# An up product in two slices at a time: four full passes and four 32-row tiles in place of eight full passes

## The chip, the cores and the metric

The kernel runs on one core of a Trainium2 chip. The metric is the device time of one execution in microseconds (us), as the median of several runs. A smaller number is better.

## What is computed

Agent attention over 4 batches of 12,480 tokens with 128 channels and 49 agents, followed by a feed-forward layer of 2,048 hidden units over all 49,920 tokens. All data are float32 (q, k and the agents are drawn eight times larger than v). Cut to what matters:

```python
a2k = softmax(scale * agents @ k.T)      # 49 x 12480 per batch
agent_v = a2k @ v                        # 49 x 128
q2a = softmax(scale * q @ agents.T)      # 12480 x 49
x = q2a @ agent_v                        # tokens x 128
h = x @ w_in                             # 128 -> 2048
g = h * sigmoid(1.702 * h)
out = g @ w_out                          # 2048 -> 128
```

## The kernel before

**What is multiplied.** The 128 channels between the attention and the feed-forward layer are never formed. For each batch the kernel computes `agent_v @ w_in` once, a 49 x 2048 matrix, and uses it as the weights of the up product; the moving operand of that product is the softmax of a token over the 49 agents. The output is computed transposed, channels on partitions.

**Two parts for each operand.** The matmuls run on the reduced type float32r. To keep float32 accuracy, each operand is split into an upper part (the value rounded to float32r) and a lower part (what is left), and a product is the sum of up to three products of parts. In the up product the split of the softmax costs no extra pass: rows 0 to 48 of the 128 contraction rows hold the upper part of 49 agents, rows 64 to 112 the lower part, and the weights `wh` are repeated in both places. Rows 49 to 63 and 113 to 127 are zero and do nothing. The lower part of the weights, `wl`, is a second pass over the same moving operand.

**Tiles.** Tokens go in groups of 960 (`GT`), two chunks of 480 (`CH`): 13 groups in each of 4 batches, 52 in all. The 2,048 hidden units go in 16 slices of 128 (`NF`). A step is one slice of one group, so there are 832 steps. In each step, on TensorE:

- `up` (L391): two accumulators `ph` of 128x480 in PSUM (of four), and four matmuls of 480 columns: `wh` with each chunk (`sa`, `sb`; L396), `wl` with each chunk (L398). ScalarE then applies GELU from each `ph` into `g` (L401).
- `high` (L404): the upper part `gh` of `g`, by a casting DMA from GpSimd's queue in 6 slices of 16 (L407), by ScalarE in 8 (L409), by VectorE in 2 (L411). `low` (L414): `gl = g - gh` on VectorE (L416).
- `down` (L419), five steps later (`LAG`): six matmuls of 480 columns into the two `po` accumulators (L427): `wo_h` with `gh`, `wo_h` with `gl`, `wo_l` with `gh`, for two chunks.

**What runs beside it.** Jobs are put at steps by hand (`put(step, job)`) and run between `up` and `down` of the step. For the next group: the query scores at steps 4 and 5 (`Q_AT`; `scores`, L181: 16 small bf16 matmuls for each half, then a VectorE reduction that adds the two halves of each score, L196), the shift by the maximum, the exponential on ScalarE at step 8 (`E_AT`, L358), the sums at 10, the softmax into `p_pad` at 11, and at step 13 (`P_AT`) `query_pairs` (L375): four transposes on TensorE (L379), then ScalarE copies the upper parts into `sa` and `sb` and VectorE writes the lower parts. For the next batch: key loads, splits and scores, the key maximum (two small transposes, L245 with 120 contraction rows and L255 with 49), then v (`value_hi`, L284, and `value_lo`, L288, on VectorE), the product with v (L292), and last `weights_part` (L329), which makes `wh` and `wl` (L335 to L337), 512 columns at a time.

**Order.** Each engine runs its instructions in program order. From step 16 on the order on TensorE, ScalarE, VectorE and GpSimd is exactly the written one. The SP queue issues all loads and stores, also in order; GpSimd's queue issues the casting DMAs.

Of the kernel before, what the change touches and what calls it, by code (L numbers as in the profile page):

```python
# [8 lines left out]
F32 = mybir.dt.float32  # L9
# [25 lines left out]
HI_ON_ACT = (0, 2, 4, 6, 7, 12, 13, 15)  # L35
# [4 lines left out]
def kernel(  # L40
# [51 lines left out]
    p_pad = []  # L92
    for i in range(2):
        t = const.tile([P, CH // TB, P], F32, name=f"p_pad{i}")
        nc.gpsimd.memset(t, 0.0)
        p_pad.append(t)


    e_sb = []
    for i in range(2):  # L100
        t = const.tile([P, KB, A + 1], F32, name=f"e_sb{i}")
        nc.gpsimd.memset(t[:, :, A:], EPS)
        e_sb.append(t)
# [77 lines left out]
    def scores(b, parts, out, c):  # L181
        x0, x1, x2 = parts
        a = ag_part[:, b].rearrange("p i a -> p (i a)")
        mm = nc.tensor.matmul
        ps = ps_m.tile([P, 512], F32, name="ps_m")
        for j in range(KB // 2):
            t0 = (c * KB // 2 + j) * TB
            t = slice(t0, t0 + P)
            o = ps[:, j * 2 * A : (j + 1) * 2 * A]
            mm(out=o, lhsT=x0[:, t], rhs=a[:, 0 : 2 * A], start=True, stop=False)  # L190
            mm(out=o[:, A:], lhsT=x0[:, t], rhs=a[:, 2 * A :], start=False, stop=False)  # L191
            mm(out=o, lhsT=x1[:, t], rhs=a[:, 0 : 2 * A], start=False, stop=False)  # L192
            mm(out=o[:, 0:A], lhsT=x2[:, t], rhs=a[:, 0:A], start=False, stop=True)  # L193
        s = ps[:TB, : KB * A].rearrange("p (j i a) -> p j a i", i=2, a=A)
        o = out[:, c * KB // 2 : (c + 1) * KB // 2, :]
        nc.vector.tensor_reduce(out=o, in_=s, axis=AX.X, op=ALU.add)  # L196
# [29 lines left out]
    def key_scores(b, g, parts, c):  # L226
        scores(b, parts, score[:TB, g * KB : (g + 1) * KB, :], c)
# [55 lines left out]
    def value_hi(g, vt):  # L283
        nc.vector.tensor_copy(out=v_pair[:TB, :, 0:C], in_=vt[:TB])  # L284
# [43 lines left out]

    def weights_part(b, w, c):  # L329
        if c == 0:  # L330
            wts[b] = wpool.tile([P, F], F32R, name="wh"), wpool.tile([P, F], F32R, name="wl")
        wh, wl = wts[b]
# [3 lines left out]
        nc.scalar.copy(out=wh[:, s], in_=pw)  # L336
        nc.vector.tensor_sub(out=wl[:, s], in0=pw, in1=wh[:, s].bitcast(F32))  # L337


    def query_load(b, g):  # L340
        t = loads.tile([P, GT + PAD], F32, name="qt", tag="qt", bufs=2)
        nc.sync.dma_start(out=t[:, 0:GT], in_=qT[b, :, g * GT : (g + 1) * GT])
        return t

    def query_scores(n, b, parts, c):
        sd = e_sb[n % 2][:TB, :, 0:A]
        scores(b, parts, sd, c)
        return sd
# [11 lines left out]
    def query_sums(n):  # L360
        z = work.tile([P, KB], F32, name="z")
        nc.vector.tensor_reduce(out=z[:TB], in_=e_sb[n % 2][:TB], axis=AX.X, op=ALU.add)
        nc.vector.reciprocal(out=z[:TB], in_=z[:TB])
        return z

    def query_softmax(n, e, z):
        pp = p_pad[n % 2]
        nc.vector.tensor_tensor(
            out=pp[:TB].rearrange("p i (c x) -> p c i x", c=2)[:, :, :, 0:A],
            in0=e.rearrange("p (c i) a -> p c i a", c=2),  # L370
            in1=z[:TB].rearrange("p (c i) -> p c i", c=2).unsqueeze(3).broadcast_to([TB, 2, KB // 2, A]),
            op=ALU.mult,
        )

    def query_pairs(g):  # L375
        pp = p_pad[g % 2]
# [7 lines left out]
        nc.scalar.copy(out=sa[0:H], in_=ps[0:H, :CH])  # L384
        nc.scalar.copy(out=sb[H:P], in_=ps[H:P, :CH])
        nc.vector.tensor_sub(out=sa[H:P], in0=ps[0:H, :CH], in1=sa[0:H].bitcast(F32))
        nc.vector.tensor_sub(out=sb[0:H], in0=ps[H:P, :CH], in1=sb[H:P].bitcast(F32))
        return sa, sb


    def up(f, wts, pairs):  # L391
        wh, wl = wts
        s = slice(f * P, (f + 1) * P)
        ph = [ps_h.tile([P, 512], F32, name="ph") for _ in range(2)]
        for c in range(2):
            nc.tensor.matmul(out=ph[c][:, :CH], lhsT=wh[:, s], rhs=pairs[c], start=True, stop=False)  # L396
        for c in range(2):
            nc.tensor.matmul(out=ph[c][:, :CH], lhsT=wl[:, s], rhs=pairs[c], start=False, stop=True)  # L398
        g = gpool.tile([P, 2, CH], F32, name="g", bufs=LAG)
        for c in range(2):  # L400
            nc.scalar.activation(out=g[:, c, :], in_=ph[c][:, :CH], func=AF.Gelu_apprx_sigmoid)  # L401
        return g

    def high(f, g):  # L404
        gh = gpool.tile([P, 2, CH], F32R, name="gh", bufs=LAG + 1)
        if f in HI_ON_DMA:
            nc.gpsimd.dma_start(out=gh, in_=g)  # L407
        elif f in HI_ON_ACT:
            nc.scalar.copy(out=gh, in_=g)  # L409
        else:  # L410
            nc.vector.tensor_copy(out=gh, in_=g)  # L411
        return gh

    def low(g, gh):  # L414
        gl = gpool.tile([P, 2, CH], F32R, name="gl", bufs=LAG - 1)
        nc.vector.tensor_sub(out=gl, in0=g, in1=gh.bitcast(F32))  # L416
        return gl

    def down(f, gp, po):  # L419
        gh, gl = gp  # L420
        for lhsT, rhs, first, last in (
# [4 lines left out]
            for c in range(2):  # L426
                nc.tensor.matmul(  # L427
                    out=po[c][:, :CH],
                    lhsT=lhsT[:, f, :],
                    rhs=rhs[:, c, :],  # L430
                    start=(f == 0 and first),
                    stop=(f == NF - 1 and last),
                )
# [15 lines left out]
    scored = {}  # L449
    sums = {}  # L450
# [27 lines left out]
    def do_key_scores(b, g, c):  # L478
        key_scores(b, g, k_parts[b, g], c)
# [9 lines left out]
    def do_query_scores(n, c):  # L489
        if n < B * NG:  # L490
            b, g = divmod(n, NG)
            scored[n] = query_scores(n, b, q_parts[n], c)
# [23 lines left out]
    def first_keys():  # L516
        tags = [("g", LAG), ("gh", LAG + 1), ("gl", LAG - 1)]
# [10 lines left out]
    for g in range(NKG):  # L528
        if g % 2 == 0:
            vt0 = wpool.tile([P, 2, KB, C + 1], F32, name="vt0", tag=("wh", "wl")[g // 2 % 2])  # L530
# [11 lines left out]
    do_query_scores(0, 0)  # L542
    do_query_scores(0, 1)
# [54 lines left out]
    for b in range(B - 1):  # L598
        s0 = b * per_batch
        for k in range(NKG):  # L600
            t = pe_step(s0 + (10 if b == 0 else K_AT) + 5 * k)
            t1 = pe_step(t + 1)
            put(t - 13 if b else max(t - 13, 0), lambda b=b, k=k: do_key_load(b + 1, k))
            for i in range(4):
                put(t - 5 + i, lambda b=b, k=k, i=i: do_key_split(b + 1, k, i))
            put(t, lambda b=b, k=k: do_key_scores(b + 1, k, 0))
            put(t1, lambda b=b, k=k: do_key_scores(b + 1, k, 1))
            put(t1 + 1, lambda k=k: key_part_max(k))
        mx = {}
        put(t1 + 2, lambda mx=mx: key_max_0(mx))  # L610
        t = pe_step(t1 + 4)
        put(t, lambda mx=mx: key_max_1(mx))
        t = pe_step(t + 3)
        put(t, lambda mx=mx: key_max_2(mx))
        shift = t + 2


        g0 = (shift + 3 - s0 - E_AT + NF - 1) // NF
        for k in range(NKG):
# [6 lines left out]
            put(t - 3, lambda b=b, k=k: value_hi(k, vts[b + 1, k]))  # L626
# [36 lines left out]
    def step(t):
        if t < steps:
            n, f = divmod(t, NF)
            g = up(f, wts[n // NG], pairs[n])
            if f == NF - 1:
                pairs.pop(n)
        for job in at.pop(t, ()):
            job()  # L670
        if t < steps:
            gh = high(f, g)

            if f in HI_ON_DMA:
                at.setdefault(t + 3, []).insert(0, lambda t=t: live.update({t: (gh, low(g, gh))}))
            else:
                live[t] = gh, low(g, gh)
        if t >= LAG:
            n, f = divmod(t - LAG, NF)
            if f == 0:  # L680
                po[n] = [ps_o.tile([P, 512], F32, name=f"po{c}") for c in range(2)]
            down(f, live.pop(t - LAG), po[n])
            if f == NF - 1:
                store(*divmod(n, NG), po.pop(n))

    for t in range(NF):
        step(t)
# [42 lines left out]
```

## Time and profile before

| | |
|---|---|
| median of 3 runs | 2118.99 us (2118.6 to 2119.08) |
| the profiled execution | 2118.66 us, of which the span of the profile is 2116.9 us |
| granted TensorE clock, mean | 0.994 |
| ScalarE busy | 1563.2 us, 74% |
| DMA issues of `gh` | 312 of 480 KB, median 2.8 us to landing |
| first matmul of the up product, last matmul | at 75.16 and 2112.0 us |

The profile is one execution on the core. A row of the timeline gives the start in us from the span's beginning, the duration, the engine (PE is TensorE's matmul, PEld its weight load, DVE is VectorE, ACT ScalarE, POOL GpSimd, SPq the SP queue), the line, the operation, output and inputs, and in brackets the idle time before and what ended it. Matmul durations overlap: the distance from start to start tells what one costs. A row of the groups gives the busy time of all instructions of a line and form, the mean of one in ns, and the idle time before them.

### The profile page before, as it was taken

To read this page: it belongs to the slowest core of one execution; us is meant where nothing else is said; L and a number is where in the kernel's file an instruction comes from. 1 tells how busy PE (TensorE), PEld (TensorE's weight loads), DVE (VectorE), ACT (ScalarE), POOL (GpSimd) and SP (SyncE) were. 2 spreads that over 40 slices of the span, in tenths; PEclk is the share of its full clock that TensorE was granted. 3 is DMA by queue.
4 is the path that set the end of the run, shared out by engine and by line. 5 is a ranking of instruction groups with operands and counts; after the bars stand their busy time and mean duration, and the time that the engine had idled before them with its cause. 6 is when DMAs were issued, how large, how long until landed. Compare 5 with 4: busy or idle time off the path is not lost.

```text
span 2116.9 us, 32655 instructions
## 1 busy us (share of the span) xinstructions
PE 2085.7 (99%) x12232; PEld 1769.1 (84%) x12232; DVE 1741.0 (82%) x2259; ACT 1563.2 (74%) x2524; POOL 195.9 (9%) x436
## 2 busy tenths in 40 slices
PE   7899999999999999999999999999999999999999
PEld 7678888888888888888888888888888888888887
DVE  6899989888789988888879998888787777777775
ACT  3566777777777777777777777777777877878786
POOL 3000000000010000000001000000000000000100
PEclk9999999999999999999999999999999999999999
DMA  9533433433333433433323443433423333232322
GB/s 266 163 125 126 154 108 122 131 122 131 112 113 131 150 122 112 131 122 126 127 103 126 146 132 111 131 122 122 131 94 103 106 109 113 103 122 94 112 94 84
DMA packets 94276, 262.01 MB, mean 124 GB/s; under 512 B 9245, under 2 KB 35165, under 8 KB 94117
## 3 DMA queue, kind: packets, MB, share of 16 engines
q0 software_dynamic: 44928, 153.37, 20.4%
q1 hardware_dynamic: 49188, 106.55, 17.7%
q8 instruction: 96, 1.57, 0.3%
q14 instruction: 64, 0.52, 0.1%
HBM read 80.97 MB, written 25.56 MB: 50 GB/s over the span
## 4 chain that ended last, share of the span: by engine, by line
PE 92%; DVE 6%; DMA 1%; issue 1%; ACT 0%; ACTq 0%; SPq 0%; DVEq 0%; POOLq 0%
PE po L427 50%; PE ph L396 16%; PE ph L398 16%; PE ps_m L292 2%; DVE gl L416 2%; PE ps_m L190 2%; PE ps_m L192 1%; PE ps_m L209 1%; PE ps_m L379 1%; PE ps_m L191 1%; PE ps_m L193 1%; PE ps_m L335 1%; DMA words<-w_out 0%; DVE rest L175 0%; DVE v_pair L288 0%
## 5 line engine op out<-in xcount | busy, mean ns | idle before, releaser
L401 ACT ACTIVATE g<-ph 128x480 f32<-128x480 f32 x1664 | 854.4, 573 | 467.6 <-PE ph L398 434.0
L416 DVE TENSOR_TENSOR gl<-g,gh 128x960 fp32r<-128x960 f32 x832 | 951.1, 1156 | 249.6 <-ACT gh L409 200.0
L427 PE MATMUL po<-gh,wo_h 128*128 128x480 f32 x1664 | 524.5, 396 | 0.2 <-ACT o L438 0.2
L427 PE MATMUL po<-gh,wo_l 128*128 128x480 f32 x1664 | 501.8, 383 | 0.0
L427 PE MATMUL po<-gl,wo_h 128*128 128x480 f32 x1664 | 498.1, 381 | 2.2 <-DVE gl L416 2.2
L409 ACT CAST gh<-g 128x960 fp32r<-128x960 f32 x416 | 415.3, 998 | 12.3
L427 PEld LDWEIGHTS po<-gl,wo_h 128*128 128x128 f32 x1664 | 313.3, 188 | 52.3 <-DVE gl L416 2.3
L427 PEld LDWEIGHTS po<-gh,wo_l 128*128 128x128 f32 x1664 | 313.7, 189 | 49.3
L407 POOL DMA_DIRECT2D gh<-g x312 | 167.8, 538 | 1836.7 <-ACT g L401 1163.5
L427 PEld LDWEIGHTS po<-gh,wo_h 128*128 128x128 f32 x1664 | 292.7, 189 | 39.9 <-issue 5.7
L396 PE MATMUL ph<-sb,wh 128*128 128x480 f32 x832 | 319.5, 384 | 0.0
L396 PE MATMUL ph<-sa,wh 128*128 128x480 f32 x832 | 318.7, 383 | 0.6 <-ACT g L401 0.4
L398 PE MATMUL ph<-sa,wl 128*128 128x480 f32 x832 | 317.5, 382 | 0.0
L398 PE MATMUL ph<-sb,wl 128*128 128x480 f32 x832 | 315.9, 380 | 0.0
L396 PEld LDWEIGHTS ph<-sb,wh 128*128 128x128 f32 x832 | 157.5, 189 | 31.7 <-ACT g L401 5.3
L396 PEld LDWEIGHTS ph<-sa,wh 128*128 128x128 f32 x832 | 157.6, 189 | 29.9 <-ACT g L401 1.0
L398 PEld LDWEIGHTS ph<-sb,wl 128*128 128x128 f32 x832 | 156.6, 188 | 25.2 <-issue 0.2
L398 PEld LDWEIGHTS ph<-sa,wl 128*128 128x128 f32 x832 | 156.5, 188 | 24.5 <-issue 0.2
L177 DVE TENSOR_TENSOR rest<-rest 128x488 bf16<-128x488 f32 (+1 forms) x182 | 130.2, 721 | 0.6
L192 PE MATMUL ps_m<-ag_part,rest 128*128 128x98 bf16 x728 | 114.9, 205 | 0.0
L193 PE MATMUL ps_m<-ag_part,rest 128*128 128x49 bf16 x728 | 111.4, 187 | 0.0
L196 DVE TENSOR_REDUCE e_sb<-ps_m 120x196 f32<-120x392 f32 x104 | 58.9, 566 | 37.0 <-PE ps_m L193 36.9
(103 smaller groups left out, 1830.9 us busy)
## 6 DMA issues: line engine op xcount, KB each, us to landing
gh<-g POOLq DMA_DIRECT2D x312, 480.0 KB, 2.8
kt<-kT SPq DMA_DIRECT2D x52, 480.0 KB, 3.7
qt<-qT SPq DMA_DIRECT2D x52, 480.0 KB, 4.4
vt<-v SPq DMA_DIRECT2D x52, 480.0 KB, 4.2
outT<-o SPq DMA_DIRECT2D x104, 240.0 KB, 2.2
words<-w_in SPq DMA_DIRECT2D x4, 512.0 KB, 11.0
words<-w_out SPq DMA_DIRECT2D x4, 512.0 KB, 8.4
ag_sb<-agT SPq DMA_DIRECT2D x1, 98.0 KB, 2.0
```

Source lines behind the costliest of these rows:

```text
L177: nc.vector.tensor_sub(out=halves(r)[1][:, s], in0=r[:, s], in1=halves(r)[0][:, s])
L190: mm(out=o, lhsT=x0[:, t], rhs=a[:, 0 : 2 * A], start=True, stop=False)
L192: mm(out=o, lhsT=x1[:, t], rhs=a[:, 0 : 2 * A], start=False, stop=False)
L193: mm(out=o[:, 0:A], lhsT=x2[:, t], rhs=a[:, 0:A], start=False, stop=True)
L196: nc.vector.tensor_reduce(out=o, in_=s, axis=AX.X, op=ALU.add)
L396: nc.tensor.matmul(out=ph[c][:, :CH], lhsT=wh[:, s], rhs=pairs[c], start=True, stop=False)
L398: nc.tensor.matmul(out=ph[c][:, :CH], lhsT=wl[:, s], rhs=pairs[c], start=False, stop=True)
L401: nc.scalar.activation(out=g[:, c, :], in_=ph[c][:, :CH], func=AF.Gelu_apprx_sigmoid)
L407: nc.gpsimd.dma_start(out=gh, in_=g)
L409: nc.scalar.copy(out=gh, in_=g)
L416: nc.vector.tensor_sub(out=gl, in0=g, in1=gh.bitcast(F32))
L427: nc.tensor.matmul(out=po[c][:, :CH], lhsT=lhsT[:, f, :], rhs=rhs[:, c, :], start=(f == 0 and first), stop=(f == NF - 1 and last),)
```

## The change

The up product is made for two slices at once, and most of the lower weights move into the rows that were zero.

- `R = 30` agents: the 15 zero rows 49 to 63 of `wh` now hold the lower weights of agents 0 to 14, the zero rows 113 to 127 those of agents 15 to 29; `sa` and `sb` hold the upper softmax of these agents there. So the pass with `wh` also makes 30 agents' products with the lower weights.
- The lower weights of the last 19 agents go into `wq`, four times over, at rows 0, 32, 64 and 96; `rq` holds the upper softmax of these agents in the same rows, chunk 0 in row groups 0 and 2, chunk 1 in 1 and 3. After the four full passes of two slices (two slices by two chunks), four matmuls with 19 rows each, at tile positions (0,0), (32,0), (64,0), (96,0), finish the four `ph`, one tile each. All four `ph` of PSUM are thus in use at once.
- The rows are filled by DMAs inside SBUF, issued by SP (`move`): eight for each group of tokens in `query_pairs`, six for each of the four `weights_part` of a batch. The product with the lower part of the softmax and the lower weights, which the old second pass made too, is left out.
- A step pair runs `up` of two slices, the jobs of the first, `high` of the first and `low` of the slice two before, `high` of the second, `down` of the odd and then the even slice four steps earlier, with the jobs of the second step and its `low` between them.
- Even slices get `gh` by DMA (8 of 16); ScalarE does 6 odd ones, VectorE slices 7 and 9.
- `scores`: ScalarE copies one half of the scores out of PSUM, and VectorE adds the other a step later (instead of one reduction by VectorE).
- `value_hi` becomes a casting DMA from DRAM on GpSimd's queue.
- Jobs are placed anew (`P_AT` 10, `E_AT` 6, `Q_AT` 2 and others), and single buffers replace pairs for `p_pad`, `e_sb` and the query loads.

```diff
-LAG = 5
+LAG = 4
+G_BUFS = 5
+GH_BUFS = 6
+GL_BUFS = 4
-Q_AT = 4
-E_AT = 8
-P_AT = 13
-S_AT = 15
-K_AT = 4
-V_AT = 1
-V2_AT = 11
+Q_AT = 2
+E_AT = 6
+P_AT = 10
+S_AT = 13
+K_AT = 3
+V_AT = 0
+V2_AT = 9
+R = 30
-HI_ON_DMA = (1, 3, 5, 10, 11, 14)
-HI_ON_ACT = (0, 2, 4, 6, 7, 12, 13, 15)
+HI_ON_ACT = (1, 3, 5, 11, 13, 15)
...
-        s = ps[:TB, : KB * A].rearrange("p (j i a) -> p j a i", i=2, a=A)
+        s = ps[:TB, : KB * A].rearrange("p (j i a) -> p j i a", i=2, a=A)
-        nc.vector.tensor_reduce(out=o, in_=s, axis=AX.X, op=ALU.add)
+        nc.scalar.copy(out=o, in_=s[:, :, 0, :])
+        return lambda: nc.vector.tensor_add(out=o, in0=s[:, :, 1, :], in1=o)
...
-    def value_hi(g, vt):
-        nc.vector.tensor_copy(out=v_pair[:TB, :, 0:C], in_=vt[:TB])
+    def value_hi(b, g):
+        nc.gpsimd.dma_start(out=v_pair[:TB, :, 0:C], in_=v[b, :, g * KB : (g + 1) * KB, :])
...
         nc.scalar.copy(out=wh[:, s], in_=pw)
-        nc.vector.tensor_sub(out=wl[:, s], in0=pw, in1=wh[:, s].bitcast(F32))
+        wl = work.tile([P, 512], F32R, name="wl")
+        nc.vector.tensor_sub(out=wl[:A], in0=pw[:A], in1=wh[:A, s].bitcast(F32))
+        move(wh[A:H, s], wl[0 : R // 2])
+        move(wh[H + A : P, s], wl[R // 2 : R])
+        for i in range(4):
+            move(wq[i * 32 : i * 32 + A - R, s], wl[R:A])
+
+    def move(out, in_):
+        nc.sync.dma_start(out=out.bitcast(F32), in_=in_.bitcast(F32))
...
+        rq = work.tile([P, CH], F32R, name="rq")
+        hi = sa[0:A], sb[H : H + A]
+        lo = sa[H : H + A], sb[0:A]
+        parts = ps[0:A, :CH], ps[H : H + A, :CH]
+        for c in range(2):
+            nc.scalar.copy(out=hi[c], in_=parts[c])
+        for c, t in enumerate((sa, sb)):
+            nc.vector.tensor_sub(out=lo[c], in0=parts[c], in1=hi[c].bitcast(F32))
+            move(t[A:H], hi[c][0 : R // 2])
+            move(t[H + A : P], hi[c][R // 2 : R])
+            for i in (c, c + 2):
+                move(rq[i * 32 : i * 32 + A - R], hi[c][R:A])
+        return sa, sb, rq
...
     def up(f, wts, pairs):
-        for c in range(2):
-            nc.tensor.matmul(out=ph[c][:, :CH], lhsT=wh[:, s], rhs=pairs[c], start=True, stop=False)
-        for c in range(2):
-            nc.tensor.matmul(out=ph[c][:, :CH], lhsT=wl[:, s], rhs=pairs[c], start=False, stop=True)
+        wh, wq = wts
+        rq = pairs[2]
+        tiles = [(i, c) for i in range(2) for c in range(2)]
+        cols = [slice((f + i) * P, (f + i + 1) * P) for i in range(2)]
+        ph = [ps_h.tile([P, 512], F32, name="ph") for _ in tiles]
+        for k, (i, c) in enumerate(tiles):
+            nc.tensor.matmul(out=ph[k][:, :CH], lhsT=wh[:, cols[i]], rhs=pairs[c], start=True, stop=False)
+        for k, (i, c) in enumerate(tiles):
+            r = slice(k * 32, k * 32 + A - R)
+            nc.tensor.matmul(
+                out=ph[k][:, :CH],
+                lhsT=wq[r, cols[i]],
+                rhs=rq[r],
+                start=False,
+                stop=True,
+                tile_position=(k * 32, 0),
+            )
...
+    def two_steps(t):
+        n, f = divmod(t, NF)
         if t < steps:
+            g[t], g[t + 1] = up(f, wts[n // NG], pairs[n])
+        jobs(t)
+        if t < steps:
+            gh[t] = high(f, g[t])
+        if 2 <= t < steps + 2:
+            gl[t - 2] = low(g.pop(t - 2), gh[t - 2])
+        if t < steps:
+            gh[t + 1] = high(f + 1, g[t + 1])
+        for i in (1, 0):
+            if t >= LAG:
+                m, f = divmod(t - LAG + i, NF)
...
+                down(f, gh.pop(t - LAG + i), gl.pop(t - LAG + i), po[m])
+            if i:
+                jobs(t + 1)
+                if t < steps:
+                    gl[t + 1] = low(g.pop(t + 1), gh[t + 1])
```

More of the change, by code (lines that the diff above doesn't have):

```diff
@@ L91 @@
     nc.gpsimd.memset(v_pair[:, :, 2 * C :].bitcast(F32), 1.0)
[L92 to L103, printed above, removed]
+    p_pad = const.tile([P, CH // TB, P], F32, name="p_pad")
+    nc.gpsimd.memset(p_pad, 0.0)
+    e_sb = const.tile([P, KB, A + 1], F32, name="e_sb")
+    nc.gpsimd.memset(e_sb[:, :, A:], EPS)
     w_in_sb = const.tile([P, F], F32, name="w_in_sb")
@@ L226, in key_scores @@
     def key_scores(b, g, parts, c):
-        scores(b, parts, score[:TB, g * KB : (g + 1) * KB, :], c)
+        return scores(b, parts, score[:TB, g * KB : (g + 1) * KB, :], c)
     def key_part_max(g):
@@ L330, in weights_part @@
         if c == 0:
-            wts[b] = wpool.tile([P, F], F32R, name="wh"), wpool.tile([P, F], F32R, name="wl")
-        wh, wl = wts[b]
+            wts[b] = wpool.tile([P, F], F32R, name="wh"), wpool.tile([P, F], F32R, name="wq")
+        wh, wq = wts[b]
         s = slice(c * 512, (c + 1) * 512)
@@ L336, in weights_part @@
         nc.scalar.copy(out=wh[:, s], in_=pw)
-        nc.vector.tensor_sub(out=wl[:, s], in0=pw, in1=wh[:, s].bitcast(F32))
+        wl = work.tile([P, 512], F32R, name="wl")
[6 more added lines that the diff above has]
+        nc.sync.dma_start(out=out.bitcast(F32), in_=in_.bitcast(F32))
     def query_load(b, g):
-        t = loads.tile([P, GT + PAD], F32, name="qt", tag="qt", bufs=2)
+        t = loads.tile([P, GT + PAD], F32, name="qt", tag="qt", bufs=1)
         nc.sync.dma_start(out=t[:, 0:GT], in_=qT[b, :, g * GT : (g + 1) * GT])
@@ L345, in query_scores @@
     def query_scores(n, b, parts, c):
-        sd = e_sb[n % 2][:TB, :, 0:A]
-        scores(b, parts, sd, c)
-        return sd
+        sd = e_sb[:TB, :, 0:A]
+        return sd, scores(b, parts, sd, c)
     def query_shift(sd):
@@ L361, in query_sums @@
         z = work.tile([P, KB], F32, name="z")
-        nc.vector.tensor_reduce(out=z[:TB], in_=e_sb[n % 2][:TB], axis=AX.X, op=ALU.add)
+        nc.vector.tensor_reduce(out=z[:TB], in_=e_sb[:TB], axis=AX.X, op=ALU.add)
         nc.vector.reciprocal(out=z[:TB], in_=z[:TB])
@@ L366, in query_softmax @@
     def query_softmax(n, e, z):
-        pp = p_pad[n % 2]
+        pp = p_pad
         nc.vector.tensor_tensor(
@@ new lines, in query_pairs @@
+        return sa, sb, rq
+    def up(f, wts, pairs):
+        wh, wq = wts
[15 more added lines that the diff above has]
+            )
+        gs = [gpool.tile([P, 2, CH], F32, name="g", bufs=G_BUFS) for _ in range(2)]
+        for k, (i, c) in enumerate(tiles):
+            nc.scalar.activation(out=gs[i][:, c, :], in_=ph[k][:, :CH], func=AF.Gelu_apprx_sigmoid)
+        return gs
@@ L404, in high @@
     def high(f, g):
-        gh = gpool.tile([P, 2, CH], F32R, name="gh", bufs=LAG + 1)
-        if f in HI_ON_DMA:
+        gh = gpool.tile([P, 2, CH], F32R, name="gh", bufs=GH_BUFS)
+        if f % 2 == 0:
             nc.gpsimd.dma_start(out=gh, in_=g)
@@ L414, in low, with down @@
     def low(g, gh):
-        gl = gpool.tile([P, 2, CH], F32R, name="gl", bufs=LAG - 1)
+        gl = gpool.tile([P, 2, CH], F32R, name="gl", bufs=GL_BUFS)
         nc.vector.tensor_sub(out=gl, in0=g, in1=gh.bitcast(F32))
         return gl
-    def down(f, gp, po):
-        gh, gl = gp
+    def down(f, gh, gl, po):
         for lhsT, rhs, first, last in (
@@ L430, in down @@
                     rhs=rhs[:, c, :],
-                    start=(f == 0 and first),
-                    stop=(f == NF - 1 and last),
+                    start=(f == 1 and first),
+                    stop=(f == NF - 2 and last),
                 )
@@ L449 @@
     scored = {}
+    adds = {}
     sums = {}
@@ L478, in do_key_scores @@
     def do_key_scores(b, g, c):
-        key_scores(b, g, k_parts[b, g], c)
+        adds[b, g, c] = key_scores(b, g, k_parts[b, g], c)
     def do_key_values(b, g):
@@ L491, in do_query_scores, with do_query_add @@
             b, g = divmod(n, NG)
-            scored[n] = query_scores(n, b, q_parts[n], c)
+            scored[n], adds[n, c] = query_scores(n, b, q_parts[n], c)
+    def do_query_add(n, c):
+        if n < B * NG:
+            adds.pop((n, c))()
     def do_query_shift(n):
@@ L529 @@
         if g % 2 == 0:
-            vt0 = wpool.tile([P, 2, KB, C + 1], F32, name="vt0", tag=("wh", "wl")[g // 2 % 2])
+            vt0 = wpool.tile([P, 2, KB, C + 1], F32, name="vt0", tag=("wh", "wq")[g // 2 % 2])
             nc.gpsimd.memset(vt0[:, :, :, C :], 1.0)
@@ L541 @@
     key_max()
-    do_query_scores(0, 0)
-    do_query_scores(0, 1)
+    for c in range(2):
+        do_query_scores(0, c)
+        do_query_add(0, c)
     do_query_shift(0)
@@ L625 @@
             put(t - 16, lambda b=b, k=k: do_value_load(b + 1, k))
-            put(t - 3, lambda b=b, k=k: value_hi(k, vts[b + 1, k]))
+            put(t - 6, lambda b=b, k=k: value_hi(b + 1, k))
             put(t - 3, lambda b=b, k=k: value_lo(k, vts.pop((b + 1, k))))
@@ L659, with jobs @@
     E = mybir.EngineType
-    live = {}
+    g = {}
+    gh = {}
+    gl = {}
     po = {}
[L663 to L668, printed above, removed]
+    def jobs(t):
         for job in at.pop(t, ()):
             job()
+    def two_steps(t):
+        n, f = divmod(t, NF)
         if t < steps:
[L672 to L687, printed above, removed]
+            g[t], g[t + 1] = up(f, wts[n // NG], pairs[n])
+            if f == NF - 2:
+                pairs.pop(n)
+        jobs(t)
[8 more added lines that the diff above has]
+                m, f = divmod(t - LAG + i, NF)
+                if f == 1:
+                    po[m] = [ps_o.tile([P, 512], F32, name=f"po{c}") for c in range(2)]
+                down(f, gh.pop(t - LAG + i), gl.pop(t - LAG + i), po[m])
[3 more added lines that the diff above has]
+                    gl[t + 1] = low(g.pop(t + 1), gh[t + 1])
+            elif t >= LAG and f == NF - 2:
+                store(*divmod(m, NG), po.pop(m))
+    for t in range(0, NF, 2):
+        two_steps(t)
     with tc.manual_schedule(engines={E.PE, E.Activation, E.DVE, E.Pool}):
-        for t in range(NF, steps + LAG):
-            step(t)
+        for t in range(NF, steps + LAG, 2):
+            two_steps(t)
     assert not at
```

34 lines of the change are left out of this document (12 added, 22 removed).

## The prediction

> **What bounds the kernel now.** I read the page's busy shares and its chain of waits first.
>
> ```profile
> span 2116.9 us, 32655 instructions
> ...
> PE 2085.7 (99%) x12232; PEld 1769.1 (84%) x12232; DVE 1741.0 (82%) x2259; ACT 1563.2 (74%) x2524; POOL 195.9 (9%) x436
> ...
> PE 92%; DVE 6%; DMA 1%; issue 1%; ACT 0%; ACTq 0%; SPq 0%; DVEq 0%; POOLq 0%
> ```
>
> TensorE carries 92% of the chain that ended last, and VectorE, the next busiest, has 2116.9 - 1741.0 = 376 us to spare. A busy share of PE alone would prove little, since durations of matmuls overlap, so I read the timeline of a step without jobs.
>
> ```profile
> 1501.10 0.38 PE L396 MATMUL ph<-sa,wh 128*128 128x480 f32 x1
> 1501.32 0.38 PE L396 MATMUL ph<-sb,wh 128*128 128x480 f32 x1
> ...
> 1503.29 0.39 PE L396 MATMUL ph<-sa,wh 128*128 128x480 f32 x1
> ```
>
> From one step's first matmul to the next one's are 2.19 us for ten matmuls of 480 columns: 0.219 each from start to start, and no gap. TensorE is saturated with full passes, so the time moves by what its queue gains or loses, until another engine is in the way.
>
> **What the change does on TensorE.** Two slices now issue eight up matmuls. The change keeps the four with `wh`, whose price stays at 0.219, and puts four 32-row tiles in place of the four with `wl`, 4 x 0.219 = 0.876 us. What the four tiles cost no row shows, but one matmul in the trace also uses only part of the rows, L255 with 49:
>
> ```profile
> 1300.29 0.38 PE L398 MATMUL ph<-sb,wl 128*128 128x480 f32 x1
> 1300.61 0.26 PE L255 MATMUL ps_m<-ident,mrow 49*120 49x49 f32 x1
> 1300.79 0.69 PE L427 MATMUL po<-gh,wo_h 128*128 128x480 f32 x2
> 1301.32 0.38 PE L427 MATMUL po<-gl,wo_h 128*128 128x480 f32 x1
> ```
>
> ```profile
> 1300.07 0.19 PEld L398 LDWEIGHTS ph<-sb,wl 128*128 128x128 f32 x1
> 1300.60 0.13 PEld L255 LDWEIGHTS ps_m<-ident,mrow 49*120 49x120 f32 x1 [0.34 <-PE ph L398]
> 1300.79 0.30 PEld L427 LDWEIGHTS po<-gh,wo_h 128*128 128x128 f32 x2
> ```
>
> and its sister L245 with 120 rows, as a control:
>
> ```profile
> 1293.61 0.38 PE L398 MATMUL ph<-sb,wl 128*128 128x480 f32 x1
> 1293.83 0.27 PE L245 MATMUL ps_m<-ident,mx 120*49 120x120 f32 x1
> 1293.86 0.68 PE L427 MATMUL po<-gh,wo_h 128*128 128x480 f32 x2
> 1294.38 0.37 PE L427 MATMUL po<-gl,wo_h 128*128 128x480 f32 x1
> ```
>
> Each stretch holds the odd matmul and three full ones (3 x 0.219 = 0.657). L245 adds 1294.38 - 1293.61 - 0.657 = 0.113 us, for 120 columns. L255 adds 1301.32 - 1300.29 - 0.657 = 0.373, with only 49 columns, which at L245's pace are 0.046. So going into a part-row form and out of it costs 0.373 - 0.046 = 0.327 us: the weight load, which normally starts with the matmul before it (1300.07), waits 0.34 for the array to run empty, and the way back waits again. The Trainium skill, "TensorEngine Tiling (Array Packing)", Key Properties, says that changing the tiling mode drains TensorE; here the trace agrees, and it speaks against a change that enters and leaves such a mode 416 times.
>
> The four tiles themselves: if they run side by side, they need one stream of 480 columns, 0.219, and whatever lies between their starts. That is unknown. Its lower end is 0. The nearest row for matmuls that each bring their own weights is in the scores:
>
> ```profile
> 1482.20 0.18 PE L191 MATMUL ps_m<-ag_part,qt 128*128 128x49 bf16 x1
> 1482.23 0.21 PE L192 MATMUL ps_m<-ag_part,rest 128*128 128x98 bf16 x1
> ```
>
> 0.03 us from start to start. The next bound is a float32 weight load: the two at 1300.79 take 0.30 with 0.19 for one, so the second starts 0.11 after the first. The upper end is no overlap, 0.219. I take 0.03, because the tiles sit in separate rows, so that a load needs no other tile's rows to be free. The block then costs 0.327 + 0.219 + 3 x 0.03 = 0.636 us, against 0.876: 0.240 less in two slices, and 416 x 0.240 = 100 us. With starts 0 apart it is 0.330 and 137 us; with 0.11 apart the block costs 0.876 and the gain is exactly nil; without any overlap it costs 0.327 + 0.876 = 1.203, a loss of 136 us.
>
> The Trainium skill, "TensorE: Matmul & The Clock Gate", Measured speedup vs the span model, gives 3.07 times for four row tiles of 32 rows and 512 columns. By it, the stream and the starts would be an estimated 4 x 0.219 / 3.07 = 0.285 in place of my 0.309, and the sum 10 us lower; no run here shows it yet.
>
> **What it does on the other engines.**
>
> ```profile
> L416 DVE TENSOR_TENSOR gl<-g,gh 128x960 fp32r<-128x960 f32 x832 | 951.1, 1156 | 249.6 <-ACT gh L409 200.0 <-PE po L427 35.5 <-DMA gh<-g 0.5
> L401 ACT ACTIVATE g<-ph 128x480 f32<-128x480 f32 x1664 | 854.4, 573 | 467.6 <-PE ph L398 434.0 <-issue 1.2 <-DVE gl L416 0.5
> ...
> L409 ACT CAST gh<-g 128x960 fp32r<-128x960 f32 x416 | 415.3, 998 | 12.3
> ...
> L196 DVE TENSOR_REDUCE e_sb<-ps_m 120x196 f32<-120x392 f32 x104 | 58.9, 566 | 37.0 <-PE ps_m L193 36.9
> ...
> L196 DVE TENSOR_REDUCE score<-ps_m 120x196 f32<-120x392 f32 x78 | 43.8, 561 | 2.7 <-PE ps_m L193 1.9
> ...
> L284 DVE CAST v_pair<-vt 120x1024 fp32r<-120x1024 f32 x39 | 26.8, 688 | 0.0
> ...
> L218 ACT COPY score<-ps_m 120x196 f32<-120x196 f32 x26 | 8.4, 322 | 19.1 <-PE ps_m L209 19.1
> ```
>
> ScalarE loses two `gh` casts of 16, 104 x 0.998 = 104 us, and gains 182 score copies of the size of L218, 182 x 0.322 = 59: 1518 us. VectorE loses L284 (26.8) and the 182 reductions (58.9 + 43.8 = 102.7); each becomes an addition of half the elements, between half of 0.566 and the whole; I take ScalarE's 0.322 for the same elements, 59: 1670 us (1714 at the upper end). Both stay under 2025, so by their sums these edits cost and bring nothing; the cover is TensorE's queue, and if it fell below 1670, VectorE would be the bound.
>
> In a step pair the four `ph` are freed by four GELUs, 4 x 0.573 = 2.3 at most, while 12 down matmuls (12 x 0.219 = 2.6) run before the next up product needs them: hidden, if ScalarE starts the GELUs at once. After the exponential it does not, and there the next bank or the transposes can be late. The even `gh`, now all by DMA, are needed one step pair (over 4 us) after they are issued.
>
> GpSimd's queue gets 104 more casting DMAs and 39 for `value_hi`. The latter waits for the product with the previous v; behind it stand the even slices' `gh` DMAs, and behind these VectorE's `low`. The v product is several steps old by then, so I price this at nothing.
>
> **The moves on SP.**
>
> ```profile
> q0 software_dynamic: 44928, 153.37, 20.4%
> q1 hardware_dynamic: 49188, 106.55, 17.7%
> ...
> outT<-o SPq DMA_DIRECT2D x104, 240.0 KB, 2.2
> ```
>
> ```profile
> 1485.26 0.34 SPq L342 DMA_DIRECT2D qt<-qT  x1
> ```
>
> Eight issues of 0.34 for each group are 2.7 us on SP; loads of k, v and q queue behind them and are due many steps later. The moves carry 15 or 19 rows, against 128 rows and 2.2 us for an `outT` store. They are issued when `query_pairs` is done, early in the pair of steps 10 and 11, and are needed at step 16: six steps of some 2.3 us (1,945 us from the first up product on, over 832 steps), 14 in all, less an up product, four GELUs and two copies (about 4.5), leave some 10 us. I take nothing for the steady state.
>
> In the prologue nothing covers them:
>
> ```profile
> 75.14 0.69 DVE L337 TENSOR_TENSOR wl<-ps_m,wh 128x512 fp32r<-128x512 f32 x1 [1.08 <-ACT wh L336]
> ```
>
> `wl` of the first 512 columns is ready at 75.83; six issues (2.0), a landing like that of `outT` (2.2) and the other moves in front of it in the queue come before the first tiles may start. Without queueing that is 4 us, with all four `wq` copies in one line behind each other (below) up to 11. I take 8, once.
>
> The sum: 2116.9 - 100 + 8 = 2025 us of span. The profiled execution took 2118.66, 1.8 more than its span, and the median of the runs is 2118.99: the forecast is **2027 us**.
>
> **The rivals.**
>
> *The tiles' weight loads follow one another (not faster).* If four float32 loads cannot overlap, the starts lie 0.11 apart, the block costs what it replaces, and the prologue's 8 us are left: 2118.7 + 8 = 2127. For it speaks that all float32 loads of the trace that follow each other at once show this 0.11; against it, that those use the same rows. It decides from 0.11 between starts upward. At 0.06, half way to my value, the gain is still 62 us, and the time 2065.
>
> *The tiles run one after another.* The block costs 1.203, the time is 2127 + 136 = 2263. The change would then not do what it says.
>
> *No draining.* If tile and full passes mix freely, the block costs 0.219 + 0.09 = 0.309, the gain is 416 x 0.567 = 236, and the time about 1891, with VectorE at 1670 close behind. L255's row speaks against it.
>
> *The moves are late.* A packet on SP's queue took on the mean 0.177 x 16 x 2116.9 / 49188 = 0.122 us. If the 19 rows of a move stay in one DMA engine, and the four `rq` moves in the same one, they take 4 x 19 x 0.122 = 9.3 and 2.2 to land, 11.5 against 10; a packet of GpSimd's queue took 0.204 x 16 x 2116.9 / 44928 = 0.154, nearly all of them rows of `gh` with 960 elements, and at half of that for 480 the moves take 5.9 + 2.2 = 8.1. Late by 1 us in each of 52 groups, the time is 2079. The Trainium skill, "DMA: Bandwidth & Descriptors", Why a DMA increments its semaphore by 16 and not by 1, says that a DMA uses the largest number of engines, up to 16, that divides its rows, so one for 19; no row here shows such a DMA.
>
> **How the numbers follow.** The forecast's case, tiles side by side with starts 0 to 0.05 apart, has 0.62, and a range of its own from 1985 (starts 0 apart, 4 us of prologue) to 2065. Loads in sequence or nearly so have 0.18, at 2075 to 2135; tiles one after another 0.07; late moves 0.07; no draining 0.06. The range 1985 to 2135 leaves out the two extreme cases, 0.13, and some of the edges. About 0.2% is what a measurement of this kernel can tell from no change. Faster by more: 0.62 + 0.07 + 0.06 = 0.75. Within 0.2%: 0.05, from the loads in sequence. Slower: the other 0.13 of these and 0.07, 0.20.
>
> **What the profile after would show.** Four tile matmuls of 19 rows after each four of `wh`, the first one's weight load idle for about 0.3 us before it, the starts of the next three a few hundredths apart, and the next full matmul some 0.64 after the usual place for the first tile. Steps without jobs of 2.07 us in the mean of two. `gh` by DMA 416 times, ScalarE near 1518, VectorE near 1670. The reasons are wrong if the tiles' starts lie 0.1 or more apart, if no idle time stands before them, if the first up product of a group waits for a DMA, or if TensorE waits for `g` or `gl` for more than some 10 us in all.

## The result and the profile after

| | before | after |
|---|---|---|
| median | 2118.8 us (2117.97 to 2119.08, 4 runs) | 2182.89 us (2176.82 to 2194.41, 4 runs) |
| profiled execution, its span | 2118.66, 2116.9 us | 2182.02, 2180.2 us |
| mean granted TensorE clock | 0.994 | 0.968 |
| ScalarE, VectorE busy | 1563.2, 1741.0 us | 1471.6, 1659.4 us |

The ratio is 1.031, with a 95% interval of 1.0267 to 1.0352: slower, and outside the range of the forecast. The page after, its busy shares and its chain of waits:

```profile
span 2180.2 us, 33873 instructions
...
PE 2055.0 (94%) x12232; PEld 1562.0 (72%) x12232; DVE 1659.4 (76%) x2220; ACT 1471.6 (67%) x2602; POOL 287.2 (13%) x577
...
PE 46%; DMA 17%; issue 10%; DVE 7%; ACT 3%; SPq 3%; POOL 1%; POOLq 0%; ACTq 0%; DVEq 0%
PE po L454 27%; DMA rq<-sb 11%; PE ph L415 8%; PE ph L418 5%; DMA gh<-g 4%; SPq L346 3%; DVE gl L443 3%; ACT g L428 2%; DMA wq<-wl 2%; PE ps_m L290 1%; PE ps_m L187 1%; PE ps_m L387 1%; DVE gh L438 1%; PE ps_m L189 1%; POOL gh L434 1%
```

TensorE's part of the chain went from 92% to 46%. DMAs hold 17%, and 11% is one small copy, `rq` from `sb`. ScalarE and VectorE have less to do than before, so neither has become the bound.

The block itself did what it was meant to do. TensorE's timeline of a step pair without jobs (a row with x4 covers four instructions):

```profile
1813.10 0.38 PE L415 MATMUL ph<-sa,wh 128*128 128x480 f32 x1
1813.32 0.38 PE L415 MATMUL ph<-sb,wh 128*128 128x480 f32 x1
1813.54 0.38 PE L415 MATMUL ph<-sa,wh 128*128 128x480 f32 x1
1813.76 0.37 PE L415 MATMUL ph<-sb,wh 128*128 128x480 f32 x1
1814.06 0.49 PE L418 MATMUL ph<-rq,wq 19*128 19x480 f32 x4
1814.48 0.71 PE L454 MATMUL po<-gh,wo_h 128*128 128x480 f32 x2
...
1817.21 0.38 PE L415 MATMUL ph<-sa,wh 128*128 128x480 f32 x1
```

All four tiles lie within 0.49 us, the length of one, and the pair takes 1817.21 - 1813.10 = 4.11 us, where the prediction had 4.14. The first tile comes 0.30 after the last full matmul instead of 0.22, and the next full matmul 0.42 after the tiles' start: the way into the tiled form and the way out of it both cost time.

At the beginning of a group it looks different. The same view, at the first step pair of a group:

```profile
1476.29 0.38 PE L415 MATMUL ph<-sb,wh 128*128 128x480 f32 x1
1476.60 0.48 PE L418 MATMUL ph<-rq,wq 19*128 19x480 f32 x1
1477.49 0.49 PE L418 MATMUL ph<-rq,wq 19*128 19x480 f32 x2 [0.41 <-DMA rq<-sb]
1479.01 0.60 PE L418 MATMUL ph<-rq,wq 19*128 19x480 f32 x1 [1.04 <-DMA rq<-sb]
1479.55 2.09 PE L290 MATMUL ps_m<-v_pair,e_pair 120*128 120x258 f32 x8
```

The second tile starts 0.89 after the first, the fourth 1.52 after the third: `rq`'s copies for the second chunk have not landed. In the 51 groups behind the first such distances between tiles beyond 0.05 us add up to 84 us, in 83 places (the expectations below count 87). In the median a group's fourth tile starts 1.68 us after its first. TensorE's waits (us in total, times, longest):

```profile
PE ph L418 <- DMA rq<-sb: 42.4, 56, 3.2
PE ps_m L387 <- DVE p_pad L376: 30.8, 28, 1.5
PE ps_m L290 <- issue: 9.8, 10, 1.9
PE ph L415 <- DMA sb<-sb: 7.4, 3, 2.6
```

(This view counts only time in which no matmul was still on record, so it has less than the 84.) The second line is another new wait: the transposes of `query_pairs` wait for the softmax.

What follows a stall is a third loss. Three stretches of 3.3 us around the one above; each line has the busy time of PE, PEld, VectorE, ScalarE and GpSimd, and the column behind them is the granted clock:

```profile
1475.90:1479.20 3.30, 1.85 (x8) 0.89 (x6) 2.56 (x4) 1.72 (x4) 0.32 (x1) 1.00 0.71 175
1479.30:1482.60 3.30, 3.30 (x12) 2.88 (x12) 1.11 (x1) 1.56 (x2) 0.11 (x1) 0.50 0.44 161
1482.70:1486.00 3.30, 3.30 (x19) 2.41 (x18) 2.73 (x3) 0.00 (x0) 0.00 (x0) 1.00 0.00 0
```

After a stretch in which TensorE was busy for 1.85 of 3.30 us, it runs at half clock for 3.4 us. There are 30 spells at half clock, 143 us in all (4 and 27 us before); half of the 116 us more is 58 us of lost work. Not every stall brings one: in 33 of the 51 groups the fourth tile starts 1.6 us or more after the first, and in 24 of these a spell begins within 5 us; in the 18 others none does.

### The profile page after: what moved, and what is told of

Its sections match the earlier page's. It is cut to its first block, busy times and chain, and to the rows that moved or that the text cites. A ratio compares the mean times of both kernels' runs of the same rounds, so it can differ in the third digit from the quotient of the medians.

```text
span 2180.2 us, 33873 instructions
## 1 busy us (share of the span) xinstructions
PE 2055.0 (94%) x12232; PEld 1562.0 (72%) x12232; DVE 1659.4 (76%) x2220; ACT 1471.6 (67%) x2602; POOL 287.2 (13%) x577
## 4 chain that ended last, share of the span: by engine, by line
PE 46%; DMA 17%; issue 10%; DVE 7%; ACT 3%; SPq 3%; POOL 1%; POOLq 0%; ACTq 0%; DVEq 0%
PE po L454 27%; DMA rq<-sb 11%; PE ph L415 8%; PE ph L418 5%; DMA gh<-g 4%; SPq L346 3%; DVE gl L443 3%; ACT g L428 2%; DMA wq<-wl 2%; PE ps_m L290 1%; PE ps_m L187 1%; PE ps_m L387 1%; DVE gh L438 1%; PE ps_m L189 1%; POOL gh L434 1%
## 5 line engine op out<-in xcount | busy, mean ns | idle before, releaser
L428 ACT ACTIVATE g<-ph 128x480 f32<-128x480 f32 x1664 | 821.9, 576 | 596.6 <-PE ph L418 586.6
L454 PE MATMUL po<-gh,wo_h 128*128 128x480 f32 x1664 | 564.2, 421 | 0.0
L454 PE MATMUL po<-gl,wo_h 128*128 128x480 f32 x1664 | 512.9, 390 | 0.0
L434 POOL DMA_DIRECT2D gh<-g x416 | 222.5, 535 | 1802.0 <-ACT g L428 1409.5
L436 ACT CAST gh<-g 128x960 fp32r<-128x960 f32 x312 | 314.3, 1007 | 6.9
L418 PE MATMUL ph<-rq,wq 19*128 19x480 f32 x1664 | 249.4, 483 | 51.2 <-DMA rq<-sb 42.4
L418 PEld LDWEIGHTS ph<-rq,wq 19*128 19x128 f32 x1664 | 97.4, 182 | 216.3 <-issue 140.4
L174 DVE TENSOR_TENSOR rest<-rest 128x488 bf16<-128x488 f32 (+1 forms) x182 | 128.7, 715 | 0.0
L194 DVE TENSOR_TENSOR e_sb<-ps_m,e_sb 120x196 f32<-120x196 f32 x104 | 37.1, 357 | 88.4 <-ACT e_sb L193 88.4
L438 DVE CAST gh<-g 128x960 fp32r<-128x960 f32 x104 | 68.2, 656 | 34.7 <-ACT g L428 34.6
L399 DVE TENSOR_TENSOR sa<-ps_m,sa 49x480 fp32r<-49x480 f32 x52 | 33.9, 651 | 58.9 <-ACT sb L397 54.9
```

Of the source, the lines that this page charges most:

```text
L174: nc.vector.tensor_sub(out=halves(r)[1][:, s], in0=r[:, s], in1=halves(r)[0][:, s])
L418: nc.tensor.matmul(out=ph[k][:, :CH], lhsT=wq[r, cols[i]], rhs=rq[r], start=False, stop=True, tile_position=(k * 32, 0),)
L428: nc.scalar.activation(out=gs[i][:, c, :], in_=ph[k][:, :CH], func=AF.Gelu_apprx_sigmoid)
L454: nc.tensor.matmul(out=po[c][:, :CH], lhsT=lhsT[:, f, :], rhs=rhs[:, c, :], start=(f == 1 and first), stop=(f == NF - 2 and last),)
```

## The experiments

Theory A: the moves into `rq` are late because a copy of 19 rows runs on one DMA engine, row by row, and the four of a group stand in line. Rival B: they are late because SP takes long to issue eight of them. Rival C: some limit of size. For the clock: it follows the stalls, or the tiles themselves lower it. The ratios are to the kernel before, with a 95% interval.

### 20 rows in place of 19

```diff
-        move(wh[H + A : P, s], wl[R // 2 : R])
+        move(wh[H + A : P - 1, s], wl[R // 2 : R - 1])
...
-            move(wq[i * 32 : i * 32 + A - R, s], wl[R:A])
+            move(wq[i * 32 : i * 32 + A - R + 1, s], wl[R - 1 : A])
...
-                move(rq[i * 32 : i * 32 + A - R], hi[c][R:A])
+                move(rq[i * 32 : i * 32 + A - R + 1], hi[c][R - 1 : A])
...
-            r = slice(k * 32, k * 32 + A - R)
+            r = slice(k * 32, k * 32 + A - R + 1)
```

> The moves into rq and wq carry 20 rows in place of 19; the weights of the added row stand in wq and are zero in wh, so that nothing is counted twice. Theory A (a move of 19 rows runs on one DMA engine, about 1.5 us each, and the four of a group wait in line): 20 rows spread over several engines, the waits of the first tiles of each group for rq (87 us between tiles in the changed kernel) fall below 15, and the time comes to about 2060, between 2040 and 2080. Rival B (the moves are late because SP needs 0.6 to 0.9 us to issue each of eight): the row count does not matter, the waits stay above 70 and the time above 2165. On the clock: if the half-speed spells (30 in the changed kernel, 4 before) follow the stalls, they fall below 12; if the tiles themselves lower the clock, they stay near 30 and the time is near 2105.

Measured: 2039.28 us, ratio 0.9635 (0.9618 to 0.9652): 144 us less than with 19 rows, and faster than the kernel before. Behind the first group no tile waits any more. Half-speed spells: 4; mean clock 0.992. TensorE's longest waits are now

```profile
PE ps_m L387 <- DVE p_pad L376: 29.0, 26, 1.5
PE ps_m L207 <- DMA kt<-kT: 5.2, 1, 5.2
PE ps_m L290 <- issue: 5.1, 7, 1.1
```

The time is just below the 2040 to 2080 that A had. What B says is partly true: SP does need longer for moves than the prediction took. Its instructions in the changed kernel (shortest, median and longest ns):

```profile
L346 SPq DMA_DIRECT2D sa<-sa x104: 788/856/1575, 60.1 to 2126.5; - x104
L346 SPq DMA_DIRECT2D rq<-sa x104: 571/618/628, 62.0 to 2128.1; - x104
L346 SPq DMA_DIRECT2D sb<-sb x104: 785/812/859, 69.1 to 2129.7; - x104
L346 SPq DMA_DIRECT2D rq<-sb x104: 572/621/1097, 70.8 to 2131.2; - x104
```

and with 20 rows:

```profile
L346 SPq DMA_DIRECT2D rq<-sb x104: 717/722/879, 69.7 to 1989.6; - x104
```

But 20 rows take longer to issue, 722 ns against 621, and are on time all the same. So B, as the cause of the waits, falls. That the tiles lower the clock falls too: the tiles are all there, and the spells are gone.

### No moves into rq

```diff
+    rq_zero = const.tile([P, CH], F32R, name="rq")
+    nc.gpsimd.memset(rq_zero.bitcast(F32), 0.0)
...
-        rq = work.tile([P, CH], F32R, name="rq")
+        rq = rq_zero
...
-            for i in (c, c + 2):
-                move(rq[i * 32 : i * 32 + A - R], hi[c][R:A])
```

> Leaves out the four moves into rq of each group; rq is zero throughout, so the products of the last 19 agents' lower weights are missing. All matmuls are issued as before. Theories A and B agree on the ceiling: no wait for rq (87 us) and few half-speed spells (some 45 us): about 2045. If 20 rows reach this within 15 us, nothing of the moves' price is left in their issue on SP. If the time stays above 2140, the waits for rq were not what costs.

Measured: 2051.87 us, 0.9685 (0.9669 to 0.9702). The ceiling was met (2045 was expected), and 20 rows reach it; they are even 13 us faster, 7 of it in the prologue, where `wq` still moves 19 rows here (the second group's first up product begins at 128.7 us, with 20 rows at 121.7), and 5 of it in the wait of the transposes for `p_pad` (34.2 us here, 29.0 with 20 rows). So nothing of the moves' price is left in their issue on SP.

### 17 and 18 rows

In the changed kernel, fewer rows into `rq` and `wq`:

```diff
-            move(wq[i * 32 : i * 32 + A - R, s], wl[R:A])
+            move(wq[i * 32 : i * 32 + A - R - 2, s], wl[R + 2 : A])
...
-                move(rq[i * 32 : i * 32 + A - R], hi[c][R:A])
+                move(rq[i * 32 : i * 32 + A - R - 2], hi[c][R + 2 : A])
...
-            r = slice(k * 32, k * 32 + A - R)
+            r = slice(k * 32, k * 32 + A - R - 2)
```

> The changed kernel with moves of 17 rows into rq and wq in place of 19; leaves out the products of two agents' lower weights. Theory A (the moves of 19 rows are slow because 19 has no divisor up to 16 but 1, so that one DMA engine does a whole move; 17 is as bad): a move still takes 17 x 0.08 = 1.35 us on its engine, the waits for rq stay above 60 us and the time above 2145. Rival C (less than 20 rows fall under some other limit, or the bytes on the queue decide): 17 rows should be no slower than 20, and the time falls below 2060.

Measured: 2115.94 us, 0.9998 (0.9985 to 1.0012), clock 0.983. Both expectations missed: slower than 20 rows by 77 us, but faster than 19 by 67. The waits between tiles add up to 56 us behind the first group, so A was right that they stay, and wrong in how much two rows less bring. At the first pair of most groups only the fourth tile waits now:

```profile
1438.17 0.38 PE L415 MATMUL ph<-sb,wh 128*128 128x480 f32 x1
1438.48 0.52 PE L418 MATMUL ph<-rq,wq 17*128 17x480 f32 x3
1440.16 0.48 PE L418 MATMUL ph<-rq,wq 17*128 17x480 f32 x1 [1.15 <-DMA rq<-sb]
```

The median distance between the third and the fourth tile is 1.34 us with 19 rows and 1.13 with 17, about 0.07 for each row in both, as it would be if the rows were copied one after the other. 18 rows (one off the 19 in the same three lines, not two) tell the theories apart:

> The changed kernel with moves of 18 rows into rq and wq; leaves out the products of one agent's lower weights. Theory A (what counts is whether the rows can be shared out: 18 = 2 x 9, 20 = 2 x 10, but 17 and 19 are prime): 18 rows are as good as 20, waits for rq under 15 us, time 2030 to 2060. Rival C (the price goes with the bytes below some limit between 19 and 20 rows): 18 rows lie between 17 and 19, about 2150.

Measured: 2038.06 us, 0.963 (0.9614 to 0.9646), and behind the first group no tile waits for `rq`. So 17 is slow, 18 fast, 19 slow, 20 fast: not the size decides but whether the row number can be shared out, and C falls. The Trainium skill, "DMA: Bandwidth & Descriptors", Why a DMA increments its semaphore by 16 and not by 1, says that a DMA runs on the largest number of engines, up to 16, that divides its rows: by it 17 and 19 rows have one engine, 18 have 9 and 20 have 10. These four runs agree with it.

The packet records of the traces show the copies themselves. From the issue of a group's last `rq` copy to the end of its last packet 5.81 us pass with 17 rows, 1.87 with 18, 6.35 with 19 and 1.82 with 20 (medians of the 51 groups behind the first). With 19 rows the packets of these copies, one of 1,920 bytes for each row, come one at a time, mostly 0.075 us apart; with 20 rows many run side by side. `gh`, by DMAs of another queue, lands later too when the row number is 17 (3.5 us) or 19, and not with 18 (3.0) or 20; with 19 rows and with 20:

```profile
gh<-g POOLq DMA_DIRECT2D x416, 480.0 KB, 3.8
```

```profile
gh<-g POOLq DMA_DIRECT2D x416, 480.0 KB, 3.1
```

### The softmax ahead of VectorE's cast

```diff
-        put(s0 + E_AT + 3, lambda n=n: do_query_softmax(n + 1))
+        put(s0 + E_AT + 2, lambda n=n: do_query_softmax(n + 1))
```

> Only the multiplication that ends the softmax is put one step earlier, ahead of VectorE's cast of slice 9. Theory: the transposes wait for p_pad (37 us) because on VectorE the softmax stands behind that cast, which waits for the GELUs behind the exponential; the wait falls below 10, the moves start up to 0.8 us earlier, and the time falls by 37 to 70 us, to about 2125. Rival: the exponential itself is late, so that the wait only changes its name, and the time stays within 15 us of 2182.

Measured: 2184.37 us, 1.0317 (1.03 to 1.0335): no gain, and yet the wait for `p_pad` is gone. TensorE's waits:

```profile
PE ph L418 <- DMA rq<-sb: 57.4, 63, 2.1
PE ph L415 <- DMA sb<-sb: 12.3, 3, 4.4
PE ps_m L290 <- issue: 10.5, 9, 1.9
```

The distances between tiles grew from 84 to 100 us, and the clock fell from 0.968 to 0.961, some 15 us of work. Together with 5 us more for `sb` this gives back what was won. The copies have less time here: from a group's first move to its next up product 8.8 us pass in place of 9.8 (medians), and the fourth tile starts 1.90 us after the first in place of 1.68. Whether that is why the clock drops more often was not tried. With both edits:

> Both the 20 rows and the early softmax. If the two waits stand one behind the other on TensorE, both gains add up: 2060 - 37 = about 2023, close to the 2027 of the prediction, and below the 2119 of before. If the early softmax only gains because it starts the moves earlier, it adds nothing to the 20 rows: about 2060.

Measured: 2005.59 us, 0.9472 (0.9458 to 0.9486): 34 us less than 20 rows alone. Where `rq` is on time, the early softmax gives back all of the 29.0 us that the transposes waited for it, and some more.

### What the other parts of the change are worth

From here on the kernel with 20 rows and the early softmax (2005.59 us) is the starting point. First the score halves, then v's upper part, on VectorE as they were before (the reduction of the scores still runs one step later than there):

```diff
-        s = ps[:TB, : KB * A].rearrange("p (j i a) -> p j i a", i=2, a=A)
+        s = ps[:TB, : KB * A].rearrange("p (j i a) -> p j a i", i=2, a=A)
...
-        nc.scalar.copy(out=o, in_=s[:, :, 0, :])
-        return lambda: nc.vector.tensor_add(out=o, in0=s[:, :, 1, :], in1=o)
+        return lambda: nc.vector.tensor_reduce(out=o, in_=s, axis=AX.X, op=ALU.add)
```

> 20 rows and the early softmax, with the score halves added by one reduction on VectorE as before. VectorE gets some 182 x 0.2 = 38 us more, ScalarE 58 us less. Theory: neither is the bound and the time stays within 6 us of 2006. Rival: the scores stand at the head of the chain over the exponential and the softmax to the transposes, so that a copy less on ScalarE starts it earlier and the time falls by 10 or more; or VectorE is close enough to its limit that the time grows by 10 or more.

Measured: 2015.96 us, 0.9523 (0.9509 to 0.9538): 10 us slower, just what the second rival asked for. VectorE's busy time is 1695.6 us in place of 1662.0. Some 6 of the 10 us lie in the clock (0.990 of 2014.3 us against 0.993 of 2003.5); what lowers it here is open. The copies on ScalarE are worth about 10 us.

```diff
-        nc.gpsimd.dma_start(out=v_pair[:TB, :, 0:C], in_=v[b, :, g * KB : (g + 1) * KB, :])
+        nc.vector.tensor_copy(out=v_pair[:TB, :, 0:C], in_=vts[b, g][:TB])
...
-            put(t - 6, lambda b=b, k=k: value_hi(b + 1, k))
+            put(t - 3, lambda b=b, k=k: value_hi(b + 1, k))
```

> 20 rows and the early softmax, with v's upper part by VectorE as before. VectorE gets 27 us more in 39 casts; GpSimd's queue loses 39 DMAs of many small rows, which stand in front of the casts of g. Theory: hidden, within 6 us of 2006. Rival: these DMAs delay gh and v_pair and so TensorE (some 8 us of waits before the product with v are left), and the time falls by 8.

Measured: 1999.36 us, 0.9442 (0.9427 to 0.9456), the fastest of the kernels that leave out nothing more than the change does. The 6 us are at the edge of what was expected either way, and the intervals of the two kernels lie only just apart; but the wait in front of the product with v (8.3 us in 9 places) is gone from the list of TensorE's waits, so the DMA of v brought at best nothing here.

### The tiles by themselves

One full matmul in place of the four tiles. It leaves out all that the tiles compute and adds one product with `wh` a second time, so only its time can be used:

```diff
-            nc.tensor.matmul(out=ph[k][:, :CH], lhsT=wh[:, cols[i]], rhs=pairs[c], start=True, stop=False)
+            nc.tensor.matmul(out=ph[k][:, :CH], lhsT=wh[:, cols[i]], rhs=pairs[c], start=True, stop=k < 3)
...
+            if k == 3:
+                nc.tensor.matmul(out=ph[k][:, :CH], lhsT=wh[:, cols[i]], rhs=pairs[c], start=False, stop=True)
-            r = slice(k * 32, k * 32 + A - R + 1)
...
-                tile_position=(k * 32, 0),
-            )
```

> 20 rows and the early softmax, with one full matmul of 128 rows in place of the four tiles, into the fourth accumulator; leaves out the last 19 agents' lower weights. The full pass costs 0.219 and nothing drains. Theory: the four tiles run side by side, and what they cost above one pass, 0.61 - 0.22 = 0.39 us in each of 416 step pairs, is the way into the tiled form and out of it: 163 us less, about 1845, less 20 to 40 of new stalls where VectorE and ScalarE are close behind: 1845 to 1885. Rival: the drain is hidden by other work, and the time stays above 1960.

Measured: 1871.56 us, 0.8837 (0.8823 to 0.885), 134 us less. A step pair without jobs:

```profile
1809.63 0.38 PE L415 MATMUL ph<-sb,wh 128*128 128x480 f32 x1
1809.85 0.38 PE L418 MATMUL ph<-sb,wh 128*128 128x480 f32 x1
1810.07 0.59 PE L447 MATMUL po<-gh,wo_h 128*128 128x480 f32 x2
...
1812.69 0.38 PE L415 MATMUL ph<-sa,wh 128*128 128x480 f32 x1
```

This pair began at 1808.97 and takes 3.72 us, 0.39 less than with tiles, as expected; 416 of them would be 162 us. Most of the rest is new idle time: TensorE's span less its busy time is 56 us here and 35 with tiles. And all four tiles in one row group:

```diff
-            r = slice(k * 32, k * 32 + A - R + 1)
+            r = slice(0, A - R + 1)
...
-                tile_position=(k * 32, 0),
+                tile_position=(0, 0),
```

> 20 rows and the early softmax, with all four tiles at the first 32 rows, each still a matmul of 20 rows with its own weights and its own accumulator; the second chunk's products of the last 19 agents' lower weights are made with the first chunk's softmax. Theory: the gain comes from the four row groups working side by side, so that now each tile takes a stream of its own, 0.22 us from start to start: 416 x 3 x 0.21 = 262 us more, about 2265, slower than before. Rival: short contractions are cheap in any place: the time stays below 2060.

Measured in a single run: 2249.88 us, 244 more, near the expected 262. Its four tiles:

```profile
1809.94 0.38 PE L415 MATMUL ph<-sb,wh 128*128 128x480 f32 x1
1810.25 1.13 PE L418 MATMUL ph<-rq,wq 20*128 20x480 f32 x4
```

They take 1.13 us, where four row groups take 0.49: (1.13 - 0.49) / 3 = 0.21 for each further tile, as much as a full matmul. So the row groups do work side by side, and the whole gain of the up product hangs on it.

## Why the prediction was wrong

**The bound: right.** TensorE's queue decided. Where its waits were removed, the time followed: 2005.59 us with 20 rows and the early softmax, 112 below before.

**The block of tiles: right.** Predicted were 0.636 us for the block and 4.14 for a pair; the pair took 4.11. The starts, taken as 0.03 apart with 0 to 0.22 as bounds, are together within 0.01. The price of the way in and the way out, worked out from the rows of L245 and L255, held nearly: 4.11 less 16 full matmuls leaves 0.61 for the block, and 0.38 of that is the two ways, where 0.327 was predicted. The two misses, 0.05 too little and 0.08 too much, in part cancel, so that 4.14 came this close is in part luck. A single full pass in place of the tiles saves 0.39 in a pair, where 0.636 - 0.219 = 0.417 was predicted. The rivals of weight loads in sequence, of tiles one after another and of no draining fall with that.

**The other engines: right within 4%.** ScalarE 1471.6 us against 1518, VectorE 1659.4 against 1670.

**The moves: the step that failed.** The prediction said "I take nothing for the steady state". It had set some 10 us of time against 8.1 to 11.5 of need, a tie within its own bounds, and called the tie zero. The time was right: 9.8 us from a group's first move to its next up product (median). The need was 11.9 us to the last packet with 19 rows, and 7.8 with 20. Two terms were mis-sized. Eight issues were priced at SP's 0.34 for a full load, 2.7 us; they take 2 x (0.86 + 0.62 + 0.81 + 0.62) = 5.8. And issuing and copying were treated as one or the other, though the last `rq` copies are issued at the very end and then come row by row, 6.35 us from the issue of the last one. The issue alone makes nothing late, as 20 rows show. In place of nothing came 84 us of waits between tiles. One of the prediction's own signs of being wrong had named it: a group's first up product that waits for a DMA. The rival "the moves are late" had the mechanism, by one engine for 19 rows, but a chance of only 0.07 and 1 us for each group where the median was 1.68.

**The clock: missing.** No part of the prediction had it. A stall of TensorE was priced at its own length. In this kernel a stall of 1.6 us or more was followed by half clock in 24 of 33 groups, mostly for 3.4 us, of which half is lost. Of the 144 us between 19 and 20 rows about 84 are waits, and the clock (0.968 of 2180.2 us against 0.992 of 2035.2) is 70 - 16 = 54.

**The transposes: seen, not priced.** The prediction named them as possibly late behind the exponential and took no cost. They waited 30.8 us, and with 20 rows 34 came back once the softmax stood in front of the cast.

**The prologue: about right** for 8 us. With 19 rows the second group's up product begins at 126.1 us instead of 115.4; with 20 rows at 121.7.

So 2182.89 against 2027: waits for `rq` 84, clock 58, transposes 31 make 173, more than the 156 between the two; the pair, 0.03 shorter than predicted where it has no jobs, brings up to 12 back, and the rest stays unassigned.

## What to carry to other kernels

A forecast with a saturated engine needs each new wait at its full price: if a transfer's need and its slack overlap within their bounds, the likeliest case is not zero, and a stall on TensorE can cost the slow clock after it on top of its own length. Before a copy of part of the rows goes on a path with little slack, give it a number of rows that divides well (18 or 20, not 17 or 19), even if a row is moved for nothing. Four small matmuls in four row groups took the time of one here, but each visit to the tiled form cost 0.39 us more than a full pass, so gather them as this kernel does.

## What was not expected of the hardware

- The time of these copies depends on the row count through its divisors: with 17, 18, 19 and 20 rows the last one took 5.81, 1.87, 6.35 and 1.82 us from its issue, and the kernel 2115.94, 2038.06, 2182.89 and 2039.28 us.
- SP needs longer to issue a copy of few rows inside SBUF (0.62 us for 19 rows, 0.72 for 20, 0.81 to 0.86 for 15) than a load of 128 rows (0.34).
- TensorE's clock halved for 3.4 us after a stretch of 3.3 us in which it was still busy for 1.85. The Trainium skill, "TensorE: Matmul & The Clock Gate", Part 1, ties the half clock to an idle window of about 3.4 us; here two waits with work between them were enough, and before the 23 spells that follow the first pair of the third or a later group TensorE was busy for 1.3 to 2.5 of the 3.4 us.
- Four tiles with weights of their own, in four row groups, started within 0.01 us of each other; nothing of the 0.11 between two float32 weight loads on the same rows was left.
